# Attention ahead of a mixture of experts: softmax sums from a column of ones, logit sums on GpSimd

## The chip, the core and the metric

One core of one Trainium2 chip runs the whole program. The metric is the device time of one execution in microseconds (us). Five engines work side by side, each through its own queue in order: TensorE (PE, its weight loads PEld), VectorE (DVE), ScalarE (ACT), GpSimd (POOL) and SyncE (SP), which issues most DMAs.

## What is computed

Three layers follow each other on 4608 tokens (8 batches of 576) of width 512: attention with keys and values averaged over groups of 8 positions, a mixture of 8 experts of which each token takes two, and a last layer. The change lies in the first and in the gate of the second:

```python
k_p = k.reshape(B, H, Sp, 8, D).mean(axis=3)       # Sp = 72, H = 8, D = 64
v_p = v.reshape(B, H, Sp, 8, D).mean(axis=3)
scores = np.matmul(q, k_p.transpose(0, 1, 3, 2)) / np.sqrt(D)
attn = np.exp(scores - np.max(scores, axis=-1, keepdims=True))
attn = attn / (np.sum(attn, axis=-1, keepdims=True) + 1e-09)
x = np.matmul(attn, v_p)                           # heads side by side: 4608 x 512
logits = x @ w_gate                                # 8 columns
noisy = logits + np.log1p(np.exp(x @ w_noise)) * noise
top2 = np.argpartition(-noisy, 2, axis=1)[:, :2]
out[mask] += top2_w * (np.maximum(x[mask] @ w1[e], 0.0) @ w2[e])
h = out @ w_in;  result = (h - np.tanh(h)) @ w_out
```

## The kernel before

`attention()` works on 36 tiles of 128 tokens. Nothing reorders its instructions: each engine runs them in the order in which the Python code emits them. The loop at L1665 goes over steps t, and in one step several tiles are at different stages: the exponentials of tile t (`st_exps`), the transposes of the weights of tile t-2 (`st_attT`), the transposes of q of tile t+2 (`st_q`), the scores and their row maxima of tile t+1 (`st_scores`), the product of the weights with V of tile t-3 (`st_av`), and the scaling of that product of tile t-4 (`st_g`).

`VB` holds V with 64 columns a head and, behind them, 16 more: V times the gate's weights `w_gate` and `w_noise`, so that one product gives a head's part of x and its part of the 16 logits, 80 columns a head. It is made once a batch by `vscale` (L1274): on VectorE the scales, the logit part (L1287) and the copies of the scale to `isc` (L1293, L1295); on GpSimd, for batches 2 to 7, the V part (L1299). GpSimd also halves K and V of later batches (L1146), for VectorE to go on with.

The exponentials run on ScalarE, eight a tile (one a head), each with the row's sum as a second result (`accum_out`), for which the trace shows a second instruction, ACTIVATION_READ_ACCUMULATOR. `st_norm` adds 1e-9 to the sums of four tiles at once and takes their reciprocals on VectorE (L1353, L1356). `st_g` then scales on VectorE: the x columns from PSUM into `xr` (L1404), which goes to memory by DMA, and the 128 logit columns into `lg` (L1412). At the end of every group of `sums` (five tiles, one of four, one of two) a VectorE sum over the heads gives `lz` (L1414). The product with V lies in one PSUM buffer, `px`, except for tiles 33 and 35, which use two others, and so two scalings each.

The gate (`gate_jobs`, L1430) works on groups of 10, 10, 9 and 7 tiles, that is when `st_g` has ended tiles 9, 19, 28 and 35, in steps 13, 23, 32 and 39. It is a generator: `tick()` emits its next VectorE operation, at fixed places between the stages of a step. Its first is `lz * isc` (L1442), its second two ScalarE operations on the result (L1443, L1444). It ends in lists of the tokens of each expert (`lists`), built by VectorE, ScalarE and TensorE.

Of the kernel before, what the change touches and what calls it, by code (L numbers as in the profile page):

```python
# [10 lines left out]
F32 = mybir.dt.float32  # L11
# [3 lines left out]
AF = mybir.ActivationFunctionType  # L15
OP = mybir.AluOpType
AX = mybir.AxisListType
# [1097 lines left out]
def attention(nc, tc, st, V):  # L1115
    q, k, v, w_gate, w_noise, noise = (V[n] for n in ("q", "k", "v", "w_gate", "w_noise", "noise"))
    B, H, S, D, N, E, DM, SP, NT, HP = (V[n] for n in ("B", "H", "S", "D", "N", "E", "DM", "SP", "NT", "HP"))
# [7 lines left out]
    ts = nc.vector.tensor_scalar  # L1125
# [18 lines left out]
    def add(e, b, nm, n, c=slice(0, 5)):  # L1144
        a = KV[b, nm]
        e.tensor_add(a[:, c, 0:n], a[:, c, 0:n], a[:, c, n:2 * n])  # L1146
# [37 lines left out]
    rowi = one.tile([128, 128], F32, name="rowi")  # L1184
    nc.gpsimd.iota(rowi, pattern=[[1, 128]], base=0, channel_multiplier=-1, allow_small_or_imprecise_dtypes=True)
    KB = [one.tile([128, 2 * HP * SP], F32, name=f"kb{i}") for i in range(2)]
    VB = [one.tile([128, 5, 3, D + 2 * E], F32, name=f"vb{i}") for i in range(2)]

    of = one.tile([128, 5, 4], F32, name="of")
    odd = one.tile([128, 5, 2], F32, name="odd")  # L1190
# [44 lines left out]
    def head_mask():  # L1235
        ts(lm, hm, float(SP), 8.0, op0=OP.is_lt, op1=OP.mult)
        ts(hm, hm, 0.0, None, op0=OP.is_ge)
        tt(hm, hm, lm, op=OP.mult)

    def prep_jobs(b, first=False):  # L1240
        tl = {}

        def k2():
            add(nc.vector, b, "k", 2)

        def k1():
            add(nc.vector, b, "k", 1)
            tl["ke"] = wk.tile([128, 5, 2, D], F32, name="ke", bufs=1)
            tt(tl["ke"], KV[b, "k"][:, :, 0:1].to_broadcast([128, 5, 2, D]), odd[:, :, :, None].to_broadcast([128, 5, 2, D]),
               op=OP.mult)  # L1250

        def v2():
            add(nc.vector, b, "v", 2)

        def v1():
            add(nc.vector, b, "v", 1)
            tl["va"] = KV[b, "v"]
            tl["vm"] = wk.tile([128, 1], F32, name="vm")
            nc.vector.tensor_reduce(tl["vm"], tl["va"][:, :, 0], axis=AX.XY, op=OP.max, apply_absolute_value=True)

        def vmaxT():
            p = ps.tile([1, 128], F32, name="pt", bufs=3)
            nc.tensor.transpose(p, tl["vm"], identf)
            q = [ps.tile([64, 4, 128], F32, name="pt", bufs=3) for _ in range(2)]
            for c in range(5):
                nc.tensor.transpose(q[c // 4][:, c % 4], tl["va"][:, c, 0], identf)
            yield
            tl["vx"] = wk.tile([1, 1], F32, name="vx")
            nc.vector.tensor_reduce(tl["vx"], p, axis=AX.X, op=OP.max)
            tl["vT"] = wk.tile([64, 5, 128], F32, name="vT", bufs=1)  # L1270
            nc.scalar.activation(tl["vT"][:, 0:4], q[0], AF.Copy)
            nc.scalar.activation(tl["vT"][:, 4], q[1][:, 0], AF.Copy)

        def vscale():  # L1274
            p = ps.tile([128, 1], F32, name="pt", bufs=3)
            nc.tensor.matmul(p, ones1, tl["vx"], start=True, stop=True)
            vg = ps.tile([128, 5, 3, 2 * E], F32, name="pt", bufs=3)
            for c in range(5):
                nc.tensor.matmul(vg[:, c].rearrange("p j e -> p (j e)"), tl["vT"][:, c],
                                 wg[:, hb[c]:hb[c] + 3].rearrange("p h e -> p (h e)"), start=True, stop=True)  # L1280
            yield
            m = wk.tile([128, 3], F32, name="vs")
            pow2(nc, m, p)
            of8 = wk.tile([128, 5, 3], F32, name="of8")
            ts(of8, hm, m[:, 2:3], None, op0=OP.mult)
            vb, bc = VB[b % 2], lambda n: of8[:, :, :, None].to_broadcast([128, 5, 3, n])
            tt(vb[:, :, :, D:], vg, bc(2 * E), op=OP.mult)  # L1287
            lo, hi = b * S, b * S + S
            t0, t1 = lo // 128, -(-hi // 128)
            for t in range(t0, t1):  # L1290
                o0, o1 = max(lo - 128 * t, 0), min(hi - 128 * t, 128)
                if o1 - o0 < 128:
                    ts(isc[o0:o1, t:t + 1], m[o0:o1, 1:2], 1.0 / 128, None, op0=OP.mult)  # L1293
            f0, f1 = -(-lo // 128), hi // 128
            ts(isc[:, f0:f1], m[:, 1:2].to_broadcast([128, f1 - f0]), 1.0 / 128, None, op0=OP.mult)  # L1295
            e, cs = (nc.gpsimd, each) if b > 1 else (nc.vector, [(0, 5)])
            for c0, c1 in cs:
                s = slice(c0, c1)
                e.tensor_tensor(vb[:, s, :, 0:D], tl["va"][:, s, 0:1].to_broadcast([128, c1 - c0, 3, D]), bc(D)[:, s], op=OP.mult)  # L1299

        def kbd():
            for i, (c0, c1) in enumerate(((0, 3), (3, 5))):
                w = cuts[c1] - cuts[c1 - 1]
                p = ps.tile([128, 4, 128], F32, name="pt", bufs=3)[:, 0:c1 - c0, 0:w]
                for c in range(c0, c1):
                    nc.tensor.transpose(p[:, c - c0], tl["ke"][:w, c].rearrange("p i d -> p (i d)"), identf[:w, :w])
                o = KB[b % 2][:, cuts[c0]:cuts[c1]].rearrange("p (c n) -> p c n", n=w)
                nc.scalar.activation(o, p, AF.Copy, scale=1.0 / 512)
            yield
        return dict(k2=k2, k1=k1, v2=v2, v1=v1, vt=vmaxT, vs=vscale, kb=kbd)  # L1310

    QT, SC, AT, ATT, PV, XT, SM, RC = {}, {}, {}, {}, {}, {}, {}, {}

    def st_q(t):
        p = ps.tile([128, HP, 128], F32, name="pt", bufs=3)
# [19 lines left out]

    def st_exps(t):
        at = wk.tile([128, 2, 4, SP], F32, name="at", bufs=3)
        if t % 4 == 0:
            SM[0] = wk.tile([128, 4, 2, 4], F32, name="sm"), t
        sm, t0 = SM[0]  # L1340
        AT[t] = at
        for g, (p, mx) in enumerate(SC.pop(t)):
            for j in range(4):
                nc.scalar.activation(at[:, g, j], p[:, j], AF.Exp, bias=mx[:, j:j + 1], accum_out=sm[:, t - t0, g, j:j + 1])
        if t % 4 == 3:
            SM[1] = sm, t0

    def st_norm(t):
        if t % 4 != 3:
            tick(2)  # L1350
            return
        sm, t0 = SM.pop(1)
        ts(sm, sm, 1e-9, None, op0=OP.add)  # L1353
        tick()
        rc = wk.tile([128, 4, H], F32, name="rc")
        nc.vector.reciprocal(rc, sm.rearrange("p t a b -> p t (a b)"))  # L1356
        for u in range(t0, t + 1):
            RC[u] = rc[:, u - t0]
        tick()

    def st_attT(t):
        at = AT.pop(t)
        a = wk.tile([128, 5, 128], F32, name="aT")
# [9 lines left out]
    def st_av(t):  # L1373
        a = ATT.pop(t)
# [3 lines left out]
            p = ps.tile([128, 2, 512], F32, name="px", bufs=1)  # L1378
            p = [p[:, 0], p[:, 1], p]
        PX[t] = p  # L1380
        n1 = D + 2 * E
        for o, n, b, s in runs(t):
            vb = VB[b % 2]
            for g, parts in enumerate((((0, 0, 2), (1, 0, 3), (2, 0, 1)), ((2, 1, 2), (3, 0, 2), (4, 0, 2)))):
# [5 lines left out]

    PX = {}
    sums = (0, 5, 10, 15, 20, 25, 29, 34)
    LG = [None, 0]

    def st_g(t):
        p, rc = PX.pop(t), RC.pop(t)
        xr = wk.tile([128, DM], F32, name="xr", bufs=3)
        r = rc.rearrange("p (g h) -> p g h", g=2)[:, :, :, None]
        n1 = 4 * (D + 2 * E)
        gs = [(slice(0, 2), p[2][:, :, 0:n1].rearrange("p g (h n) -> p g h n", h=4))] if len(p) == 3 else \  # L1400
            [(slice(g, g + 1), p[g][:, 0:n1].rearrange("p (g h n) -> p g h n", g=1, h=4)) for g in range(2)]
        for g, x in gs:
            m = x.shape[1]
            tt(xr.rearrange("p (g h n) -> p g h n", g=2, h=4)[:, g], x[:, :, :, 0:D], r[:, g].to_broadcast([128, m, 4, D]), op=OP.mult)  # L1404
        nc.sync.dma_start(x_d[128 * t:128 * t + 128, :], xr)
        if t in sums:
            LG[0] = wk.tile([128, 5, 2, 4, 2 * E], F32, name="lg", bufs=2)
            LG[1] = t
        lg, t0 = LG
        for g, x in gs:  # L1410
            m = x.shape[1]
            tt(lg[:, t - t0, g], x[:, :, :, D:], r[:, g].to_broadcast([128, m, 4, 2 * E]), op=OP.mult)  # L1412
        if t + 1 in sums or t + 1 == NT:
            nc.vector.tensor_reduce(lz[:, t0:t + 1], lg[:, 0:t + 1 - t0].rearrange("p t g h e -> p t e (g h)"),  # L1414
                                    axis=AX.X, op=OP.add)

    def psum(shape):
        return ps.tile(shape, F32, name="pt", bufs=3)
# [116 lines left out]
    def tick(n=1):  # L1535

        while pend and n and held[0] != "pe":
            n -= 1
            if held[0]:
                held[0] -= 1  # L1540
            else:
                step_gate()
# [122 lines left out]
    for t in range(NT + 4):  # L1665
# [7 lines left out]
        if t >= NT:  # L1673
            warm(4, "psc")
        if 0 <= t - 1 < NT:
            st_norm(t - 1)
        if 0 <= t - 4 < NT:
            st_g(t - 4)
            if t - 4 in groups:
                pend.append(gate_jobs(*groups[t - 4]))  # L1680
        tick()
        if 0 <= t - 2 < NT:
            st_attT(t - 2)
        if t + 2 < NT:
            st_q(t + 2)
        tick()
# [73 lines left out]
```

## Time and profile before

| | us |
|---|---|
| median of 3 runs (lowest to highest) | 1770.16 (1767.76 to 1774.76) |
| the profiled execution | 1768.31 |
| its span, from first to last instruction | 1766.5 |
| busy in it: TensorE, weight loads | 1724.0, 1037.9 |
| busy in it: VectorE, ScalarE, GpSimd | 1285.0, 922.6, 277.0 |

Times in the rows count from the start of the span. The attention stage is the first 217 us or so; the first matmul of the experts on gathered tokens starts at 217.16. A busy time is the time covered by an engine's records; records of one engine overlap a little, so the spacing of starts says more of what a short operation costs than its own time. Where an instruction waited, the row says for which engine and line.

### The profile page before, as it was taken

The page shows a single profiled execution, that of the slowest core. Times are in us where ns is not written, and L with a number is a line of the kernel's source. Part 1 is how long each engine was busy: PE and PEld are TensorE (multiplying, and loading weights), DVE is VectorE, ACT ScalarE, POOL GpSimd, SP SyncE. Part 2 cuts the span into 40 slices and gives each one's busy share as a digit, 9 for nine tenths or more (in the row PEclk, how much of TensorE's full clock was granted, in tenths as well). Part 3 has the DMA queues.
Part 4 walks back from the last instruction along what each step waited for, and adds up shares of the span by engine and source line. Part 5 has one row for each costly group of instructions (what it writes and reads, how often), then busy time and mean ns, then how long its engine had stood idle before and what let it go on. Part 6 is the DMA issues. An engine that isn't in the chain of part 4 may idle for free. (4 is left out here: it accounts for less than half of the span.)

```text
span 1766.5 us, 28298 instructions
## 1 busy us (share of the span) xinstructions
PE 1724.0 (98%) x10456; PEld 1037.9 (59%) x10456; DVE 1285.0 (73%) x2566; ACT 922.6 (52%) x2229; POOL 277.0 (16%) x291
## 2 busy tenths in 40 slices
PE   8988899999999999999999999999999999999998
PEld 6988744455454545545454544666666666666664
DVE  7899867766667676666564558688787879788765
ACT  6887624434343443424243356466575757666554
POOL 3343113022030301101010111012020101110000
PEclk9999999999999999999999999999999999999999
DMA  9967334644755565554553435242231414131100
GB/s 249 274 174 199 97 101 133 164 129 138 223 135 158 139 146 149 140 134 123 155 144 81 125 94 147 55 90 69 46 93 39 88 27 96 36 79 53 33 25 26
DMA packets 264127, 203.44 MB, mean 115 GB/s; under 512 B 188129, under 2 KB 208609, under 8 KB 263969
## 3 DMA queue, kind: packets, MB, share of 16 engines
q1 hardware_dynamic: 251808, 162.16, 34.8%
q0 software_dynamic: 11904, 38.81, 8.5%
q8 instruction: 87, 1.43, 0.3%
q14 instruction: 72, 0.58, 0.1%
q10 hardware_dynamic: 256, 0.46, 0.1%
HBM read 121.82 MB, written 45.74 MB: 95 GB/s over the span
## 5 line engine op out<-in xcount | busy, mean ns | idle before, releaser
L360 ACT ACTIVATE hT<-ph 128x512 f16<-128x512 f32 (+2 forms) x192 | 96.9, 505 | 438.8 <-PE ph L358 427.9
L356 PE MATMUL ph<-xTp,pair 128*128 128x384 f16 (+2 forms) x736 | 245.5, 334 | 1.1 <-PEq L456 0.6
L357 PE MATMUL ph<-xTp,pair 128*128 128x384 f16 (+2 forms) x736 | 245.0, 333 | 1.6 <-issue 1.6
L358 PE MATMUL ph<-xTp,pair 128*128 128x384 f16 (+2 forms) x736 | 245.1, 333 | 0.0
L361 DVE SCALAR_TENSOR_TENSOR hT<-ph,hT 128x512 f16<-128x512 f32 (+2 forms) x192 | 110.8, 577 | 179.5 <-ACT hT L360 176.1
L1047 PE MATMUL py<-wo,gT 128*128 128x512 f16 x576 | 218.4, 379 | 1.0 <-issue 1.0
L1045 PE MATMUL py<-wo,gT 128*128 128x512 f16 x576 | 218.4, 379 | 0.1
L379 PE MATMUL py<-pair,hT 128*128 128x512 f16 x576 | 218.4, 379 | 0.0
L1046 PE MATMUL py<-wo,gT 128*128 128x512 f16 x576 | 218.4, 379 | 0.0
L380 PE MATMUL py<-pair,hT 128*128 128x512 f16 x576 | 218.4, 379 | 0.0
L378 PE MATMUL py<-pair,hT 128*128 128x512 f16 x576 | 218.4, 379 | 0.0
L904 PEld LDWEIGHTS <-wi 128*128 128x128 f16 x1536 | 150.2, 98 | 59.0 <-DMA y<-yp 0.9
L315 POOL DMA_INDIRECT xg<-x_d,idx x75 | 78.7, 1050 | 667.2 <-DVE xp L342 510.3
L718 POOL DMA_INDIRECT y<-y_d,ridx x64 | 78.8, 1232 | 519.0 <-DVE y L729 240.7
L356 PEld LDWEIGHTS <-pair 128*128 128x128 f16 x768 | 75.3, 98 | 76.3 <-issue 15.8
L357 PEld LDWEIGHTS <-pair 128*128 128x128 f16 x768 | 75.4, 98 | 58.7 <-issue 2.9
L358 PEld LDWEIGHTS <-pair 128*128 128x128 f16 x768 | 75.4, 98 | 57.0 <-issue 1.1
L1004 ACT ACTIVATE th<-th,bias 128x512 f32<-128x512 f32 x144 | 102.5, 711 | 3.3 <-DVE th L1002 1.6
L1005 DVE SCALAR_TENSOR_TENSOR th<-th,t 128x512 f32<-128x512 f32 x144 | 98.8, 686 | 1.4 <-ACT th L1004 1.4
L1001 DVE SCALAR_TENSOR_TENSOR t<-hb,cinf,hs 128x512 f32<-128x512 f32 x64 | 48.0, 750 | 70.8 <-ACT hs L1000 68.7
L994 DVE TENSOR_TENSOR gT<-th,gT 128x512 f16<-128x512 f32 x144 | 98.9, 687 | 0.2 <-ACT gT L993 0.2
L1047 PEld LDWEIGHTS <-gT 128*128 128x128 f16 x576 | 56.3, 98 | 69.3 <-issue 1.5
(317 smaller groups left out, 3429.3 us busy)
## 6 DMA issues: line engine op xcount, KB each, us to landing
stage<-in_moe_w SPq DMA_DIRECT2D x64, 512.0 KB
y_d<-ys SPq DMA_DIRECT2D x82, 256.0 KB
x_d<-xr SPq DMA_DIRECT2D x36, 256.0 KB
out<-o SPq DMA_DIRECT2D x36, 256.0 KB
qt<-in_q SPq DMA_DIRECT2D x32, 256.0 KB
raw<-in_moe_w_in SPq DMA_DIRECT2D x32, 256.0 KB
raw<-in_moe_w_out SPq DMA_DIRECT2D x32, 256.0 KB
kt<-in_k SPq DMA_DIRECT2D x7, 768.0 KB
```

The costliest lines, as they stand in the source:

```text
L356: nc.tensor.matmul(p[:, :nt], w[:, 0, m, s], x[:, 0, m, :nt], start=(m == 0), stop=False)
L357: nc.tensor.matmul(p[:, :nt], w[:, 0, m, s], x[:, 1, m, :nt], start=False, stop=False)
L358: nc.tensor.matmul(p[:, :nt], w[:, 1, m, s], x[:, 0, m, :nt], start=False, stop=(m == KD - 1))
L361: stt(h[:, 1, :nt], p[:, :nt], 0.0, h[:, 0, :nt], op0=OP.max, op1=OP.subtract)
L378: nc.tensor.matmul(p, h[:, 0, s], w[:, 0, f], start=(f == 0), stop=False)
L379: nc.tensor.matmul(p, h[:, 0, s], w[:, 1, f], start=False, stop=False)
L380: nc.tensor.matmul(p, h[:, 1, s], w[:, 0, f], start=False, stop=(f == KF - 1))
L904: nc.tensor.matmul(p, w[:, a, m], y[:, c, b, m], start=(start and m + x == 0), stop=(m == 1 and x == 2), skip_group_check=True)
L1004: nc.scalar.activation(q, q, AF.Square, bias=bias[:, 2:3], scale=SP5)
L1045: nc.tensor.matmul(p, g[:, 0, s], wo[:, 0, f], start=(f == 0), stop=False)
L1046: nc.tensor.matmul(p, g[:, 0, s], wo[:, 1, f], start=False, stop=False)
L1047: nc.tensor.matmul(p, g[:, 1, s], wo[:, 0, f], start=False, stop=(f == KF - 1))
```

## The change

V's buffer gets an 81st column a head, which holds one where the row belongs to the head: the product with V then gives the sum of a row's exponentials beside x and the logits. The exponentials run without `accum_out`, `st_norm` goes, and `st_g` adds 1e-9 and takes the reciprocals for each tile by itself, reading the sums from PSUM. ScalarE copies the unscaled logit columns into `lg` (`st_lg`, which comes after `st_attT`), and GpSimd scales those of a whole group of `sums` with the reciprocals kept in `rc` and adds up the eight heads by halves. Tiles 34 and 35 are scaled and summed on VectorE as before. The copies to `isc` go to GpSimd. A group of the gate is put in the list after `st_lg`.

```diff
-    VB = [one.tile([128, 5, 3, D + 2 * E], F32, name=f"vb{i}") for i in range(2)]
+    VB = [one.tile([128, 5, 3, D + 2 * E + 1], F32, name=f"vb{i}") for i in range(2)]
...
+        for vb in VB:
+            ts(vb[:, :, :, D + 2 * E:], hm[:, :, :, None], 0.125, None, op0=OP.mult)
...
-                    ts(isc[o0:o1, t:t + 1], m[o0:o1, 1:2], 1.0 / 128, None, op0=OP.mult)
+                    nc.gpsimd.tensor_scalar(isc[o0:o1, t:t + 1], m[o0:o1, 1:2], 1.0 / 128, None, op0=OP.mult)
...
-            ts(isc[:, f0:f1], m[:, 1:2].to_broadcast([128, f1 - f0]), 1.0 / 128, None, op0=OP.mult)
+            nc.gpsimd.tensor_scalar(isc[:, f0:f1], m[:, 1:2].to_broadcast([128, f1 - f0]), 1.0 / 128, None, op0=OP.mult)
...
-                nc.scalar.activation(at[:, g, j], p[:, j], AF.Exp, bias=mx[:, j:j + 1], accum_out=sm[:, t - t0, g, j:j + 1])
+                nc.scalar.activation(at[:, g, j], p[:, j], AF.Exp, bias=mx[:, j:j + 1])
...
-        n1 = D + 2 * E
+        n1 = D + 2 * E + 1
...
     def st_g(t):
+        if t in sums:
+            LG[0:3] = [wk.tile([128, 5, 8 * n], F32, name=s, bufs=2) for s, n in (("lg", 2 * E), ("rc", 1))] + [t]
+        t0 = LG[2]
+        sm = wk.tile([128, H], F32, name="sm")
+        rc = LG[1][:, t - t0]
...
+        for g, x in gs:
+            ts(two(sm)[:, g], x[:, :, :, D + 2 * E:], 1e-9, None, op0=OP.add)
+        nc.vector.reciprocal(rc, sm)
...
+    def st_lg(t):
+        gs, r = LX.pop(t)
+        lg, rc, t0 = LG
+        o = lg[:, t - t0].rearrange("p (g h e) -> p g h e", g=2, h=4)
+        n = t + 1 - t0
+        done = t + 1 in sums or t + 1 == NT
+        last = t >= sums[-1]
+        for g, x in gs:
+            y = x[:, :, :, D:D + 2 * E]
+            if last:
+                tt(o[:, g], y, r[:, g].to_broadcast([128, x.shape[1], 4, 2 * E]), op=OP.mult)
+            else:
+                nc.scalar.activation(o[:, g], y, AF.Copy)
+        if done and last:
+            nc.vector.tensor_reduce(lz[:, t0:t + 1], lg[:, 0:n].rearrange("p t (h e) -> p t e h", h=H), axis=AX.X, op=OP.add)
+        elif done:
+            l, add = lg.rearrange("p t (h e) -> p (t h) e", h=H), nc.gpsimd.tensor_add
+            nc.gpsimd.tensor_tensor(l[:, 0:H * n], l[:, 0:H * n],
+                                    rc.rearrange("p t h -> p (t h)")[:, 0:H * n, None].to_broadcast([128, H * n, 2 * E]), op=OP.mult)
+            for h in (4, 2):
+                add(lg[:, 0:n, 0:2 * E * h], lg[:, 0:n, 0:2 * E * h], lg[:, 0:n, 2 * E * h:4 * E * h])
+            add(lz[:, t0:t + 1], lg[:, 0:n, 0:2 * E], lg[:, 0:n, 2 * E:4 * E])
...
         if 0 <= t - 1 < NT:
-            st_norm(t - 1)
+            tick(2)
         if 0 <= t - 4 < NT:
             st_g(t - 4)
-            if t - 4 in groups:
-                pend.append(gate_jobs(*groups[t - 4]))
         tick()
         if 0 <= t - 2 < NT:
             st_attT(t - 2)
+        if 0 <= t - 4 < NT:
+            st_lg(t - 4)
+            if t - 4 in groups:
+                pend.append(gate_jobs(*groups[t - 4]))
```

## Rows read from the trace of the kernel before

**Rows 1.** Stretches: length, then busy PE, PEld, DVE, ACT, POOL, clock, DMA share, GB/s.

```profile
30.00:70.00 40.00, 39.95 (x320) 37.48 (x319) 33.31 (x73) 34.81 (x178) 20.20 (x27) 1.00 1.05 278
70.00:190.00 120.00, 106.11 (x840) 98.33 (x839) 110.43 (x276) 94.42 (x449) 44.87 (x64) 0.97 0.68 185
190.00:210.00 20.00, 20.00 (x165) 18.53 (x164) 16.74 (x56) 13.68 (x53) 3.28 (x5) 1.00 0.26 93
...
250.00:1766.50 1516.50, 1499.63 (x8835) 850.95 (x8833) 1074.02 (x2008) 755.86 (x1474) 201.91 (x176) 1.00 0.40 103
```

**Rows 2.** Waits from 70 to 190 us: who waited for whom, total, times, longest.

```profile
ACT at L1344 <- DVE mx L1331: 9.9, 8, 3.8
...
PE px L1387 <- DVE lg L1412: 6.3, 4, 3.6
...
PE pt L1276 <- ACT aT L1370: 2.4, 2, 1.7
```

**Rows 3.** Stretches of a lower granted clock, the first and the last of three.

```profile
85.40:88.90 3.50, 3.50 (x16) 3.32 (x15) 2.47 (x8) 1.18 (x8) 3.33 (x7) 0.51 0.99 314
...
215.20:222.00 6.80, 4.84 (x12) 1.80 (x13) 3.41 (x11) 0.83 (x1) 0.00 (x0) 0.50 0.35 117
```

**Rows 4.** Groups by line, 0 to 218 us: busy, mean ns, idle before.

```profile
L1356 DVE RECIPROCAL rc<-sm 128x32 f32<-128x32 f32 x9 | 3.1, 347 | 0.2
...
L1353 DVE TENSOR_SCALAR sm<-sm 128x32 f32<-128x32 f32 x9 | 2.6, 291 | 0.0
...
L1295 DVE TENSOR_SCALAR isc<-vs 128x4 f32<-128x4 f32 x8 | 2.3, 286 | 0.1
...
L101 DVE TENSOR_SCALAR vs<-pt 128x1 f32<-128x1 f32 x8 | 1.2, 150 | 0.0
...
L1272 ACT ACTIVATE vT<-pt 64x128 f32<-64x128 f32 x8 | 2.1, 259 | 0.0
```

**Rows 5.** Timeline of VectorE in step 13: start, length.

```profile
76.92 0.68 DVE L1404 TENSOR_TENSOR xr<-px,rc 128x512 f32<-128x512 f32 x1
77.52 0.28 DVE L1412 TENSOR_TENSOR lg<-px,rc 128x128 f32<-128x128 f32 x1
77.83 1.25 DVE L1414 TENSOR_REDUCE lz<-lg 128x80 f32<-128x640 f32 x1
```

**Rows 6.** Timeline of GpSimd around step 23.

```profile
118.16 5.70 POOL L1146 TENSOR_TENSOR kt<-kt 128x256 f32<-128x256 f32 x5 [0.64 <-DMA kt<-in_k]
138.92 2.37 POOL L1299 TENSOR_TENSOR vb<-vt,of 128x192 f32<-128x192 f32 x5 [15.06 <-PE pt L1369]
141.26 3.46 POOL L1146 TENSOR_TENSOR vt<-vt 128x256 f32<-128x256 f32 x5
```

**Rows 7.** Timeline of ScalarE and TensorE in step 13, in brackets the wait before.

```profile
74.44 0.32 ACT L1344 ACTIVATE at<-psc,mx 128x72 f32<-128x72 f32 x1 [0.72 <-DVE mx L1331]
74.66 0.19 ACT L1344 ACTIVATION_READ_ACCUMULATOR at<-psc,mx 128x1 f32 x1
...
76.82 0.77 ACT L1370 ACTIVATE aT<-pt 128x384 f32<-128x384 f32 x2
...
78.60 1.88 PE L1387 MATMUL px<-vb,aT 128*128 128x160 f32 x12
...
83.50 0.38 PE L1276 MATMUL pt<-vx,onec 1*128 1x1 f32 x2 [0.74 <-ACT aT L1370]
```

**Rows 8.** Timeline of VectorE and TensorE around the second and third gate group.

```profile
135.72 1.22 DVE L1414 TENSOR_REDUCE lz<-lg 128x80 f32<-128x640 f32 x1
...
144.75 1.34 DVE L1146 TENSOR_TENSOR vt<-vt 128x640 f32<-128x640 f32 x1 [0.62 <-POOL vt L1146]
...
149.67 4.63 PE L1387 MATMUL px<-vb,aT 128*64 128x160 f32 x24 [3.56 <-DVE lg L1412]
...
185.98 1.04 DVE L1414 TENSOR_REDUCE lz<-lg 128x64 f32<-128x512 f32 x1
```

**Rows 9.** The group of the products with V, 0 to 218 us.

```profile
L1387 PE MATMUL px<-vb,aT 128*128 128x160 f32 (+5 forms) x456 | 72.9, 319 | 6.3 <-DVE lg L1412 6.3
```

## What is predicted

> **What bounds the kernel now.** I read first the busy time of each engine by stretches [rows 1]. From 250 us on, TensorE is busy 1499.6 of 1516.5 us with work the change doesn't touch, so only the attention stage, some 217 us, can move. From 30 to 70 us TensorE is busy 39.95 of 40 us: freeing another engine there gains nothing. From 70 to 190 us VectorE is busy 110.4 of 120 us, TensorE 106.1 and ScalarE 94.4: VectorE is the fullest, and TensorE stands still for about 14 us. From 190 to 210 us TensorE is full again. The list of waits of the middle stretch [rows 2] says what ends these 14 us: 6.3 us wait for the logit product of VectorE (L1412, which frees the one `px` buffer), 2.4 us (two waits) for ScalarE's copy L1370; the rest are smaller pieces. So a microsecond off VectorE between 70 and 190 us is worth up to a microsecond; off ScalarE, a part of 2.4 us; elsewhere nearly nothing. Last the granted clock: in three spells TensorE ran at 1.2 instead of 2.4 GHz, two of 3.4 us and one of 6.8 us [rows 3]; each 3.4 us spell costs 1.7 us of full-speed work.
>
> **VectorE, removed.** The mean times are in [rows 4], the spacing of starts in [rows 5]. A logit product ends 0.20 us after the x product before it (77.80 against 77.60): it holds the engine 0.20 us. Those of 34 of the 36 tiles go (the last two keep theirs): 6.9 us. Of eight sums L1414 seven go, six of 1.25 us and one of 1.04 [rows 5, 8]: 8.5 us. The batched add and reciprocal, 9 x (0.29 + 0.35): 5.7 us. The scale copies L1295 and L1293, which go to GpSimd, 8 x (0.29 + about 0.15, as L101): 3.5 us. In all 24.6 us.
>
> **VectorE, added.** Each tile gets its own add and reciprocal on 8 columns, two adds where the PSUM buffer is split (tiles 33 and 35). The add is nearest to L101, one column from PSUM, 0.15 us, 0.18 with the gap of a dependent one. The reciprocal lies between 0.15 (one column) and 0.35 (32 columns); a quarter of the way up, with the gap, 0.24. 38 x 0.18 + 36 x 0.24 = 15.5 us; from both sides, at 0.15 each 11 us, at 0.29 and 0.35 (the 32-column times) 23.6 us. Without the sums, 16.1 go and 15.5 come: nothing per tile. So VectorE's gain is the seven sums, and it comes in steps of 1.25 us, one every five tiles.
>
> **The new wait.** Three of these seven (tiles 9, 19, 28) close a group of the gate, and the next VectorE operation after them is `lz * isc` (L1442). Now VectorE stands at it until ScalarE has copied the tile's logits and GpSimd has done four dependent operations: 640 columns multiplied, then 320, 160 and 80 added. GpSimd's prices [rows 6]: 192 columns with a broadcast operand take 2.37/5 = 0.47 us, 256 added 3.46/5 = 0.69, and 5.70/5 = 1.14 where VectorE worked beside them. By the first the 1200 columns make 3.0 us, by the last 5.3; I take 3.2, the undisturbed rows with the hand-overs, since VectorE itself stands still meanwhile (in the third group 960 columns, 2.6).
>
> The Trainium skill ("GPSIMD Engine Reference", When to use GPSIMD, Engine selection) speaks against this move: two-input elementwise work belongs on VectorE, GpSimd being about half as fast. Its 2.6 cycles an element at 1.2 GHz would make 2.6 us of the 1200 columns before dispatch, an estimate; the rows agree with the direction, and the sum by it would be half a microsecond lower a group.
>
> Group 1, in step 13 [rows 5, 7]: the copies L1370 start at 76.82 and last 0.77, the logit copy after them some 0.26 (a 128-column copy, L1272), so GpSimd starts at about 77.95 and is done by 81.2; VectorE has ended its x product by 78.0 (76.92 + 0.42 + 0.68). L1442, which followed the sum that ended at 79.08, starts at 81.3: 2.2 us later, 3.3 us of standing. Behind it on VectorE lie the maxima of tile 14. ScalarE waits too: L1443 in its queue needs the same result, and behind that are the exponentials of tile 14, which free the score banks, and the copies for which TensorE already waited 0.74 us at 83.50. TensorE has no cover: +2.2.
>
> Group 2, in step 23: VectorE's sum starts at 135.72 and ends at 136.94 [rows 8]. GpSimd is idle until 138.92 [rows 6], so by the same steps L1442 starts at 138.7: +1.7. This delay runs on through GpSimd's queue: `vb` (138.92), then the five adds at 141.26, for which VectorE waited at 144.75 [rows 8]; the scale copies now on GpSimd add some 0.3 before `vb`. From there VectorE arrives late at L1412, for which TensorE stood 3.56 us at 149.67. +2.0 in all.
>
> Group 3, in step 32: the sum started at 185.98 and took 1.04 us [rows 8]; L1370 ends at about 187.0 and GpSimd at 190.0, so L1442 is 2.5 us late. There TensorE is full (190 to 210 us), and VectorE has pauses; I charge 0.5. Between the groups one sum goes without a wait, in steps 18 and 28: -1.25 each. That of step 8 lies where TensorE is full: 0. That of step 37 is balanced by adds and reciprocals of the last three tiles, done before in one batch at 202 us: 0.
>
> **ScalarE.** The 288 reads of the accumulator go. Eight exponentials with them span 76.82 - 74.44 = 2.38 us, while a read starts 0.22 after its exponential [rows 7]; 8 x 0.22 = 1.76 us leaves 0.6 us a tile, less 0.26 for the logit copy. Most exponentials start the moment the maximum is there (9.9 us of waits [rows 2]), so ScalarE is not the limit; the two TensorE waits on L1370 [rows 2] shrink by 0.6 each: -1.2.
>
> **TensorE.** Each head is 81 columns instead of 80: 1.25% of 72.9 us [rows 9] and of the 3.8 us in the last buffers, +0.9. **The `px` buffer** is freed by ScalarE too, after the copies L1370 of the same step; the product with V started 0.6 us or more after these in nearly all steps (78.60 against 77.59 in step 13 [rows 7]), the copy needs 0.26, and ScalarE is earlier: 0. The two mask operations at the start lie where VectorE waits for scores: 0. GpSimd's other four sums come in steps where it waits anyway: 0.
>
> **Sum.** 2.2 + 2.0 + 0.5 - 2.5 - 1.2 + 0.9 = +1.9, of which 0.3 is given back by faster logit hand-over in group 2 and 3 (ScalarE's exponentials end 0.6 earlier there): +1.6. The profiled execution took 1768.31 us (span 1766.5), the median is 1770.16, 1.85 more: 1769.9 for such an execution, 1771.8 as a median.
>
> **Rivals.**
> *The waits are covered* (0.18). If GpSimd's chain is near 2 us, or the gate's first operation finds its result ready, VectorE loses nothing and keeps three more sums. Then: -2.5 - 3 - 1.2 + 0.9, and with the small operations at 0.15 another -2.5 (20 of 36 tiles lie in the stretch it bounds), one clock spell less -1.7: 1760 to 1766. For it: VectorE is what TensorE waits for. Against: GpSimd's own rows allow no chain under 3 us.
> *The waits are long* (0.17). GpSimd works at its disturbed price, 5.3 us a chain: +2.1 for each of three groups, little of it covered, and the delayed `vb` and adds keep VectorE waiting; with small operations nearer 0.3 (+4 in the stretch bounded by VectorE) and one more clock spell (+1.7) the time is 1778 to 1784. It decides from a chain of about 4.5 us. For it: the five adds at 118.16 took 5.70 us beside VectorE's work. Against: VectorE is idle in just these chains. The Trainium skill ("SBUF — State Buffer", SBUF: two separate sides) says that a VectorE operation with two SBUF inputs and a GpSimd operation that reads SBUF exclude each other for a whole instruction; the row at 118.16 agrees with it, and the other four sums, which meet a working VectorE, would be slowed so.
> *It doesn't free VectorE at all* (0.05): a reciprocal of 8 columns costs what one of 32 does; 8 us come on VectorE, about 4.5 of them in its stretch: 1776.
>
> **How the numbers follow.** The forecast itself has 0.60, with 1768 to 1776 as its own spread. Half a per cent, 8.9 us, is about what a measurement of this kernel tells from no change. The first rival passes that bound in less than half of its cases: faster 0.07. The second in most: slower 0.13. The same: 0.80. The range takes in most of both: 1763 to 1782.
>
> **What would show it.** After: on VectorE a pause of about 3 us before each of the first three L1442, ended by GpSimd; four GpSimd operations of together 3 us a group, at seven places; no sums of 1.25 us but one short one; adds of about 0.15 and reciprocals of 0.2 us, 36 tiles of them; exponentials following each other at about 0.22 us. It would be wrong if L1442 starts with no pause, if TensorE's pauses between 70 and 190 us move away from 14 us by more than 5, or if a clock spell comes or goes.

## The result and the profile after

The changed kernel takes 1785.75 us (median; 1784.89 without one disturbed run, which the comparison leaves out), the kernel before 1768.41 us beside it: ratio 1.0086, 95% interval 1.0067 to 1.0104, or about 15 us more (12 to 18). The prediction was 1771.8 us, 1763 to 1782, so the time lies above the range. The profiled execution took 1786.61 us with a span of 1784.8, against 1768.31 and 1766.5. Of the signs that were to show the prediction wrong two came: TensorE's pauses between 70 and 190 us grew from 13.9 to 19.7 us, by more than 5, and a spell of the lower clock came, four from 70 us on instead of three.

First by stretches, in the columns of [rows 1]; the stretch from 70 us to the first matmul of the experts is shown for both kernels. After:

```profile
30.00:70.00 40.00, 39.04 (x309) 36.28 (x309) 33.07 (x72) 29.94 (x111) 24.72 (x33) 1.00 0.97 264
70.00:190.00 120.00, 100.31 (x759) 90.99 (x759) 98.64 (x245) 75.33 (x261) 58.72 (x87) 0.94 0.64 181
70.00:236.00 166.00, 137.80 (x1057) 124.64 (x1056) 135.08 (x359) 100.61 (x342) 72.29 (x106) 0.95 0.54 155
250.00:1784.80 1534.80, 1516.01 (x8924) 858.78 (x8922) 1088.94 (x2061) 760.66 (x1481) 202.73 (x176) 1.00 0.40 104
```

Before, the same stage:

```profile
70.00:218.00 148.00, 129.88 (x1029) 119.46 (x1028) 134.90 (x354) 109.47 (x502) 48.15 (x68) 0.97 0.60 166
```

The experts start 18 us later (235.25 against 217.2 us), and what lies behind their start takes 1549.6 us in this profile and 1549.4 in that of before: between these two the loss is all in the attention stage. VectorE, which the change was to free, does as much there as before, 135.1 against 134.9 us, and stands still for 30.9 us instead of 13.1. TensorE stands 28.2 instead of 18.1 us. It is also busy 7.9 us longer; about 3 of these are work that a later start pushed past 70 us, and the granted clock was 0.95 on the mean instead of 0.97. GpSimd's work went from 48 to 72 us.

Who waited for whom after, from 70 to 236 us (total, times, longest), against [rows 2]:

```profile
ACT lg L1414 <- DVE xr L1396: 16.0, 13, 6.1
...
DVE lz L1450 <- POOL lz L1423: 10.6, 3, 3.7
...
ACT g_th L1451 <- DVE lz L1450: 9.2, 3, 3.2
...
PE px L1370 <- ACT lg L1414: 7.7, 4, 5.1
PE pt L1521 <- DVE l_row L1516: 7.6, 4, 3.4
...
DVE vt L1146 <- POOL vt L1146: 2.0, 1, 2.0
```

The first two did not exist before; the third was 3.2 us in two waits. The second is the stop that the prediction priced. The first is one that it did not see: ScalarE's logit copy waits for VectorE's x product, although both only read the one `px` buffer. Held by it are `px` itself and all that is queued on ScalarE behind the copy. That TensorE waits 7.7 us for `px` instead of 6.3 is not by itself the copy's price: `e4_ones_only`, which has no such copy, shows 8.5 (below).

VectorE's groups of the stage (columns as [rows 4]):

```profile
L1392 DVE RECIPROCAL rc<-sm 128x8 f32<-128x8 f32 x36 | 7.3, 203 | 1.2
L1391 DVE TENSOR_SCALAR sm<-px 128x8 f32<-128x8 f32 x34 | 5.4, 159 | 11.6 <-PE px L1370 11.4
...
L1450 DVE TENSOR_TENSOR lz<-lz,isc 128x160 f32<-128x160 f32 (+1 forms) x3 | 1.0, 321 | 10.6 <-POOL lz L1423 10.6
```

The add and the reciprocal last about what was forecast (0.16 and 0.20 us). Step 13, the place of [rows 5, 7], from the timelines of the three engines:

```profile
80.10 0.69 DVE L1396 TENSOR_TENSOR xr<-px,rc 128x512 f32<-128x512 f32 x1
84.46 0.33 DVE L1450 TENSOR_TENSOR lz<-lz,isc 128x160 f32<-128x160 f32 x1 [3.67 <-POOL lz L1423]
...
80.83 0.28 ACT L1414 ACTIVATE lg<-px 128x128 f32<-128x128 f32 x1 [0.66 <-DVE xr L1396]
...
84.82 0.27 ACT L1451 ACTIVATE g_th<-lz 128x80 f32<-128x80 f32 x1 [3.23 <-DVE lz L1450]
...
81.18 1.28 POOL L1419 TENSOR_TENSOR lg<-lg,rc 128x640 f32<-128x640 f32 x1 [4.35 <-ACT lg L1414]
82.54 1.46 POOL L1422 TENSOR_TENSOR lg<-lg 128x320 f32<-128x320 f32 x2
84.08 0.35 POOL L1423 TENSOR_TENSOR lz<-lg 128x80 f32<-128x80 f32 x1
```

The chain is the one forecast: GpSimd needs 3.25 us (81.18 to 84.43), VectorE stands 3.67 us, ScalarE 3.23. The delay against before grows in steps: the products with V are 3 us late up to tile 10, 6 to 9.4 at tiles 14 to 18, 11 to 14 at tiles 21 to 24, 16 at tiles 30 to 35.

### The profile page after: what moved, and what is told of

It reads as the page before. It is cut to its first block, busy times and chain, and to the rows that moved or that the text cites. A ratio compares the mean times of both kernels' runs of the same rounds, so it can differ in the third digit from the quotient of the medians.

```text
span 1784.8 us, 28071 instructions
## 1 busy us (share of the span) xinstructions
PE 1727.8 (97%) x10456; PEld 1039.9 (58%) x10456; DVE 1283.5 (72%) x2566; ACT 906.6 (51%) x1976; POOL 305.7 (17%) x335
```

## The experiments

A kernel's excess is its ratio less one, times 1768 us, in the form excess [interval]; the change itself has +15 [12, 18]. "Start" is the first matmul of the experts in a profile: 217.2 us before, 235.2 after. The two measures need not agree: what lies behind the start took 1545.7 to 1552.9 us in the profiles of kernels that don't touch it, 1547.7 to 1549.6 in three of the kernel before. So where they differ, both are given.

**The column of ones alone.** `e4_ones_only` leaves logits and sums on VectorE.

```diff
-        last = t >= sums[-1]
+        last = True
```

> Only the first part of the change: sums of the softmax by the column of ones, an add and a reciprocal for each tile, the scale copies on GpSimd; the logit columns are scaled and summed by VectorE for all tiles, as before the change. Neither ScalarE's copy nor GpSimd's sums are there. If these two carry the loss, the time is that of the kernel before within 5 us (1764 to 1774). If the adds and reciprocals of each tile and the 81st column cost what is lost, it stays above 1780.

Measured: 1777.42 us, +10 [7, 13], start 225.87. A large part of the loss, 10 of 15 us by the ratios and 8.7 of 18.1 by the starts, comes without GpSimd's sums and without ScalarE's copy.

**Without most of the adds and reciprocals.** `e7_ones_one_reciprocal` is that kernel with one pair for each block of tiles.

```diff
-        rc = LG[1][:, t - t0]
+        rc = LG[1][:, 0]
...
-        for g, x in gs:
+        if t == t0:
+            for g, x in gs:
```

> The first part alone (column of ones, logits on VectorE), but the add and the reciprocal are done for the first tile of every group of tiles alone and used for all of them: 28 of 36 pairs are left out, so the output isn't scaled rightly. It takes 28 x 0.43 = 12 us off VectorE. If the small operations are what the first part costs, the time falls from 1777.4 to that of before, give or take 2 us (1766 to 1770), or below. If the 81st column, the exponentials without sums or the start cost it, it falls by under 3 us.

Measured: 1771.73 us, +2 [0, 5], start 222.35. The 28 pairs that are gone are 28 x (0.16 + 0.20 + 0.07 of gaps) = 12 us of VectorE, and they cost 7.6 us by the ratios (uncertain by some 4) and 3.5 by the starts. What is left has 5.8 us less on VectorE than the kernel before (batched add and reciprocal 5.7 and scale copies 3.5 gone, eight pairs of 0.43 come), and is no faster for it; but its scale copies bring a wait of their own, as is shown further down.

**The wider buffer.** `e6_before_pad` is the kernel before with 128 unused bytes, `e12_change_pad` the changed one with 384.

```diff
+    pad = one.tile([128, 32], F32, name="pad")
```

> The kernel before, with 128 unused bytes a partition laid behind V's buffers, as much as the 81st columns take there; no instruction changes. In all five profiles with the wider buffer TensorE waits 4.8 to 5.7 us for the loads of q at the start, against 3.0 in the one profile before. If the place of the buffers behind them slows those loads, the waits are about 5 us here too and the time rises by about 2 us. If not (chance in the one profile before, or another part of the change), they stay near 3 us and the time is that of before within 1 us.

> The changed kernel with 384 unused bytes a partition behind V's buffers, so that together with the 81st columns the buffers behind lie 512 bytes further than before the change instead of 128. If the place of the buffers slows the loads at the start, TensorE waits about 3 us for q there, as before, and the time falls by about 2 us (1783 to 1784). If the place has no part in it, the wait stays at 4.8 us or more, and the time too.

Measured: 1771.05 us, +2 [0, 4], start 220.89; and 1785.15 us, +15 [11, 20], start 233.97. So e6 and e7 agree: all that e7 changes adds up to no more than an idle pad does. At the very start TensorE waits 5.7 us for `q` after, in two pieces, and 3.1 in `e12_change_pad`; the two pieces after:

```profile
21.04 1.11 PE L1320 MATMUL pt<-identf,qt 128*128 128x128 f32 x4 [4.32 <-DMA qt<-in_q]
...
27.94 0.63 PE L1320 MATMUL pt<-identf,qt 128*128 128x128 f32 x4 [1.40 <-DMA qt<-in_q]
```

The shorter wait gained nothing in the time, so the wait for `q` is not the cause by itself.

**Repeats.** `e15_before_again` and `e16_before_again2` are the kernel before, `e17_change_again` and `e18_change_again2` the changed one, each once more.

> The kernel before, unchanged, profiled once more. If TensorE's wait for q at the start (3.0 us in the one profile before, 4.2 to 5.7 in most others, 1.5 in one) belongs to the kernel, it is within 0.5 us of 3.0 again. If it varies from execution to execution, it is not. The same for the spells of low clock: four before, of together 17 us up to the start of the experts.

> As the one above, a third profile of the kernel before: wait for q at the start within 0.5 us of 3.0 if it belongs to the kernel, spread by over 1 us if it varies.

> The changed kernel, unchanged, profiled once more. If the wait for q at the start (5.7 us) and the spells of low clock (24 us in all) belong to the kernel, they come again within 0.5 and 3.4 us; the start of the experts is then again 18 us later than before, within 2.

> As the one above, a third profile of the changed kernel: 5.7 us of waiting for q and 24 us of low clock if they belong to the kernel; the three stops before the gate, 3.2 to 3.7 us each, come again in any case.

Measured: 1768.95 and 1768.97 us, starts 217.5 and 219.4; 1790.79 and 1786.76 us, starts 236.1 and 234.7. The later start by 15 to 19 us is there in every pair. The stretches of lower granted clock are not: up to 10 us past the experts' start they add up to 17.1, 17.1 and 27.3 us before and 23.9, 41.0 and 27.3 after, and the profile with 41 us starts the experts only 0.9 us later than the one with 23.9. The wait for `q` varies too, 0.7 to 3.0 us before and 3.6 to 5.7 after.

**The gate's sums off GpSimd.** `e10_gate_sums_vectore` lets VectorE scale and sum for tiles 9, 19 and 28, and leaves GpSimd the other four sums.

```diff
-        if done and last:
+        if done and t in (9, 19, 28):
+            l = lg.rearrange("p t (h e) -> p (t h) e", h=H)
+            tt(l[:, 0:H * n], l[:, 0:H * n],
...
+            nc.vector.tensor_reduce(lz[:, t0:t + 1], lg[:, 0:n].rearrange("p t (h e) -> p t e h", h=H), axis=AX.X, op=OP.add)
+        elif done and last:
```

> The changed kernel, but the scaling and sum of the three groups that the gate reads at once (tiles 9, 19 and 28) is done by VectorE; the other four stay on GpSimd. VectorE's three stops of 3.2 to 3.7 us give way to 2.05 us of work each. If the stops cost as the attention stage of the kernel with the later gate says (6 us), a part of 3 to 5 us comes back and the time is 1778 to 1781. If a stop and the same time of work cost the same, it is 1782 to 1784.

Measured: 1780.16 us, +9 [6, 13], start 230.42; no stop before `lz * isc`. The three stops cost 4.8 us by the starts, 5.8 by the ratios, more than the three times 1.94 us of work that VectorE does in their place.

**The gate one step later.** `e2_gate_one_step_later` gives the chain a step of time.

```diff
-            if t - 4 in groups:
-                pend.append(gate_jobs(*groups[t - 4]))
+            u = t - 4 if t - 4 == NT - 1 else t - 5
+            if u in groups:
+                pend.append(gate_jobs(*groups[u]))
```

> The changed kernel, with one edit: a group of the gate (but the last) is put in the list one step, some 5 us, later, so that GpSimd's sums are ready before VectorE reads them. If the three stops of VectorE (3.67, 3.67 and 3.21 us) are what costs, they are gone and the time falls by 5 to 8 us. If ScalarE's copy behind VectorE is what costs, the time moves by less than 3 us, and ScalarE's waits for the x product stay at 15 to 20 us.

Measured: 1783.19 us, +15 [11, 18]. The stops are gone, and the experts start 6.5 us earlier than after. But the rest takes 1553.5 us instead of 1549.6; 3.23 us of it are a wait for the gathered tokens (`xg`) that the changed kernel doesn't have. From its timeline of TensorE:

```profile
228.73 0.58 PE L356 MATMUL ph<-x0T,pair 128*128 128x512 f16 x1 [6.53 <-DVE lg L1412]
...
272.63 0.63 PE L333 MATMUL pt<-identf,xg 128*128 128x128 f32 x4 [3.23 <-DMA xg<-x_d,idx]
```

**The logit copy on VectorE.** `e1_copy_vectore` copies the raw logits there and leaves the rest of the change.

```diff
-                nc.scalar.activation(o[:, g], y, AF.Copy)
+                nc.vector.tensor_copy(o[:, g], y)
```

> The changed kernel, with one edit: the unscaled logit columns are copied from PSUM by VectorE instead of ScalarE. Theory A (ScalarE's copy has to wait for VectorE's x product out of the same PSUM buffer, 18.5 us in 16 waits, and holds back everything behind it on ScalarE and the release of px): these waits are gone, TensorE's waits for the copy (7.7 us) become shorter ones for VectorE, and in spite of 0.2 us a tile more on VectorE the time falls by 4 to 9 us of the 17 lost. Theory B (the three stops of VectorE before the gate, and its operations slowed beside GpSimd's sums, are the whole loss): VectorE has 7 us more to do and the time stays or rises, 0 to +5 us.

Measured: 1783.10 us, +16 [13, 19], start 234.39: no difference. Handing the logit columns from VectorE to ScalarE was worth nothing. ScalarE's wait at the copy has only moved to its next place on VectorE, the maxima (waits from 70 to 235 us):

```profile
ACT at L1343 <- DVE mx L1333: 14.0, 13, 3.9
...
PE px L1370 <- DVE lg L1414: 7.4, 4, 4.0
```

**All sums on VectorE.** `e3_sum_vectore` keeps ScalarE's copy and gives GpSimd none of the seven sums.

```diff
-            nc.gpsimd.tensor_tensor(l[:, 0:H * n], l[:, 0:H * n],
...
+            tt(l[:, 0:H * n], l[:, 0:H * n],
...
+            nc.vector.tensor_reduce(lz[:, t0:t + 1], lg[:, 0:n].rearrange("p t (h e) -> p t e h", h=H), axis=AX.X, op=OP.add)
```

> The changed kernel, with one edit: the scaling and the sum over heads of a group of tiles are done by VectorE (one multiplication of 640 columns, about 0.8 us, and the sum of 1.25 us) and not by GpSimd. It puts 7 x 2 = 14 us on VectorE. If the wait for GpSimd and the slowing of VectorE's operations beside GpSimd are the loss, both are gone: VectorE's stops before the gate vanish, and the time falls by 2 to 6 us net of the 14. If ScalarE's copy is the loss, VectorE is later still, its copies wait longer, and the time rises by 3 to 10 us.

Measured: 1787.92 us, +22 [18, 26], start 233.1. Against `e4_ones_only` this kernel has nearly the same work on VectorE (141.6 and 139.2 us from 70 us to the experts), and is 10.5 us slower in the median (7.2 by the starts). The two differ in two things: ScalarE copies the logits, and scaling and sum come in one burst of 2 us. TensorE's waits from 45 us on, first in `e3_sum_vectore`, then in `e4_ones_only`:

```profile
PE px L1370 <- ACT lg L1414: 7.7, 4, 5.1
PE pt L1519 <- DVE l_row L1514: 7.4, 3, 4.1
PE pt L1278 <- ACT aT L1353: 3.0, 1, 3.0
...
PE pt L1268 <- ACT qT L1322: 1.9, 2, 1.6
PE pt L1268 <- ACT g_e L1469: 1.1, 1, 1.1
PE pt L1352 <- ACT vT L1273: 1.1, 1, 1.1
```

```profile
PE px L1370 <- DVE lg L1412: 8.5, 4, 5.1
PE pt L1521 <- DVE l_row L1516: 5.6, 4, 3.1
...
PE pt L1278 <- ACT aT L1353: 2.6, 1, 2.6
...
PE pt L1352 <- ACT vT L1273: 0.6, 1, 0.6
```

`px` itself is not waited for longer; the new waits are for what stands behind the copy in ScalarE's queue (`qT`, `g_e`, `vT`). How the loss divides between that queue and the burst was not separated. Beside `e10_gate_sums_vectore` it says something else: the two differ only in four of the sums, some 8 us of VectorE's work, which there are GpSimd's, and e10 is faster by 12.6 us by the ratios, 7.8 by the medians, 2.7 by the starts. With ScalarE's copy in place, taking these sums off VectorE did pay, by an amount that is not settled.

**GpSimd busy for nobody.** `e8_ones_idle_sums` is `e4_ones_only` with the four operations of seven sums done on a buffer that nobody reads.

```diff
+    LS = one.tile([128, 5, 16 * E], F32, name="ls")
...
+            if t < sums[-1]:
+                l, add = LS.rearrange("p t (h e) -> p (t h) e", h=H), nc.gpsimd.tensor_add
```

> The first part alone, and beside it GpSimd does the four operations of each of seven sums on a buffer of its own, whose result nobody reads; the real sums are VectorE's. It adds to the first part only GpSimd's being busy: VectorE's operations beside it, and what waits in GpSimd's queue. If VectorE's being slowed beside GpSimd (0.17 us operations that took 1.23 us) carries a large part of the loss, the time rises by 3 to 6 us over the first part alone (1777.4). If it carries little, by less than 1.5 us.

Measured: 1778.97 us, +8 [5, 12], start 231.29. In the profile the stage is 5.4 us longer than in `e4_ones_only`; in the time the two can't be told apart (1.6 us by the medians, none by the ratios), since the part behind came out 3.9 us shorter. VectorE's and GpSimd's operations around step 18, first in `e4_ones_only`, then here:

```profile
103.94 4.13 POOL L1146 TENSOR_TENSOR vt<-vt 128x256 f32<-128x256 f32 x5 [6.04 <-PE pt L183]
...
111.26 0.83 DVE L1251 TENSOR_TENSOR ke<-kt,odd 128x640 f32<-128x640 f32 x1
112.00 1.28 DVE L159 SCALAR_TENSOR_TENSOR pair<-stage,wsc,pair 128x1024 f16<-128x1024 f32 x1
...
113.42 0.57 DVE L1513 TENSOR_TENSOR l_one<-slot,g_col 128x800 f16<-128x800 f16 x1
```

```profile
111.26 5.57 POOL L1146 TENSOR_TENSOR vt<-vt 128x256 f32<-128x256 f32 x5
...
112.66 1.24 DVE L1251 TENSOR_TENSOR ke<-kt,odd 128x640 f32<-128x640 f32 x1
113.83 1.74 DVE L159 SCALAR_TENSOR_TENSOR pair<-stage,wsc,pair 128x1024 f16<-128x1024 f32 x1
...
116.24 1.02 DVE L1524 TENSOR_TENSOR l_one<-slot,g_col 128x800 f16<-128x800 f16 x1
```

What VectorE meets here are not the added operations but GpSimd's old additions L1146, which come 7 us later here, behind the added ones, and meet VectorE at work.

**Work taken off the kernel before.** `e9_before_four_sums` moves four sums and the scale copies to GpSimd; `e14_before_no_sums` takes the accumulator reads off ScalarE and leaves out the softmax's sums.

```diff
-                nc.scalar.activation(at[:, g, j], p[:, j], AF.Exp, bias=mx[:, j:j + 1], accum_out=sm[:, t - t0, g, j:j + 1])
+                nc.scalar.activation(at[:, g, j], p[:, j], AF.Exp, bias=mx[:, j:j + 1])
```

> The kernel before, with two parts of the change alone, those for which nothing waits at once: the sums over heads of tiles 4, 14, 24 and 33 are done by GpSimd (three adds by halves, of columns that VectorE has scaled as before), and the scale copies are GpSimd's. It takes 5 + 3.4 us off VectorE without a column of ones, a copy by ScalarE or a stop before the gate. If VectorE's work is what counts and GpSimd's costs nothing, the time falls by 3 to 6 us below that of before (1763 to 1766). If VectorE's operations are slowed beside GpSimd by as much, it is that of before within 2 us.

> The kernel before without the sums of the exponentials: no accum_out, so no reads of the accumulator, and the sums' buffer is set to a constant by GpSimd once in four tiles; the softmax isn't divided by its sums. It gives ScalarE back 0.6 us a tile and changes nothing else. By the prediction's step on ScalarE the time falls by 1 to 2 us. If ScalarE bounds more than the waits say, it falls by 4 us or more.

Measured: 1769.83 us, +1 [-2, 3], start 219.59; and 1771.04 us, +3 [0, 6], start 218.2. Neither gains, though e9 has some 8.4 us less on VectorE. No kernel of the study beats the one before.

## Why the prediction was wrong

**The account.** By the ratios, +2 up to the buffer and the column (e7, and e6 with the pad alone), +7.6 for an add and a reciprocal in every tile (e4 less e7), +5.3 for logits and sums on ScalarE and GpSimd (the change less e4): 15. Each of the two differences is uncertain by some 4 us, as the intervals give it. The profiles' starts, 222.35, 225.87 and 234.7 to 236.1 us, order the three in the same way, but make the second part 3.5 us and the third 9 to 10. So both parts are there, and which is the larger is not settled.

**The step that failed** is "16.1 go and 15.5 come: nothing per tile". Both amounts are right as lengths, and VectorE's busy time in the stage is the same. But the 15.5 us cost: the 12 of them that e7 leaves out are worth 3.5 to 7.6. What was taken off gained nothing that could be measured: the logit products 6.9 us (e1), batched add, reciprocal and scale copies 9.2 us (e7, e9), ScalarE's reads (e14, where -1.2 was forecast). Full busy time had been read as if each microsecond counted the same, 110.4 of 120 [rows 1]. Why the pairs cost and the rest doesn't pay stays open. An add and a reciprocal stand ahead of the x product, and TensorE waits until logits and x product have left `px`; but from e7 to e4 the wait for `px` grows by 0.9 us only (7.6 to 8.5), as much as those for the lists, for `idx` and for the copies `aT` do (about 1 us each). No run moved the same work from one place to the other.

**The scale copies hide a cost.** Around step 24 VectorE waits for GpSimd's additions 0.62 us in all five profiles in which the scale copies are VectorE's, and 1.3 to 4.8 us in eleven of the twelve in which they are GpSimd's; TensorE's wait for `px` that follows is 3.55 to 3.81 and 4.01 to 5.13 us. (The twelfth, `e17_change_again`, has 0.62 and 3.64.) The copies stand ahead of `vb` in GpSimd's queue, as the prediction says; it put 0.3 us on that. So e7 and e9 don't show that work off VectorE is worth nothing: a gain of one or two microseconds may be hidden behind this wait.

**"The `px` buffer: 0" failed too.** The copy's own time was right (0.28 us, 0.26 forecast); that it must wait for VectorE's x product was missed: 16.0 us in 13 waits. The Trainium skill ("PSUM — Partial Sum Buffer", PSUM bank collisions raise a hardware error) says that two engines may not touch one bank in the same partitions at once, two readers included, and that the compiler orders them. The 13 waits agree: two readers of `px` run one after the other. By that rule the logit copy stays in VectorE's chain whichever engine does it, and e1, which gives it back to VectorE, measures no difference.

**Stops: right in size.** Before `lz * isc` VectorE stood 3.67, 3.67 and 3.21 us (forecast: 3.3 in step 13). Their cost was put at 4.7 us and comes out at about 5 (4.8 to 5.8 in e10, beyond the work that takes their place there; 6.5 in e2, by the start). That the second delay runs on through GpSimd's queue is not shown. VectorE does wait for GpSimd's late additions, 2.00 us instead of 0.62 [rows 8], and TensorE 5.10 instead of 3.56 us:

```profile
156.33 1.34 DVE L1146 TENSOR_TENSOR vt<-vt 128x640 f32<-128x640 f32 x1 [2.00 <-POOL vt L1146]
...
161.79 1.61 PE L1370 MATMUL px<-vb,aT 128*64 128x162 f32 x4 [5.10 <-ACT lg L1414]
```

But `e4_ones_only`, where no stop comes before, has the same two waits, and e10 has them too:

```profile
148.38 1.33 DVE L1146 TENSOR_TENSOR vt<-vt 128x640 f32<-128x640 f32 x1 [1.99 <-POOL vt L1146]
...
153.88 5.51 PE L1370 MATMUL px<-vb,aT 128*64 128x162 f32 x24 [5.11 <-DVE lg L1412]
```

**The sums of steps 18 and 28 (-2.5)** were to be pure gain. GpSimd's operations meet a VectorE at work, and both get longer. What is left of the gain no run shows by itself: e9 has them, two more and the scale copies on GpSimd and gains nothing, and e10 gains by its four against `e3_sum_vectore`. Step 18 after:

```profile
113.00 1.28 POOL L1419 TENSOR_TENSOR lg<-lg,rc 128x640 f32<-128x640 f32 x1 [12.15 <-ACT lg L1414]
...
113.09 1.23 DVE L1494 TENSOR_TENSOR g_e<-g_e,g_hi 128x20 f32<-128x20 f32 x1
...
114.36 2.42 POOL L1422 TENSOR_TENSOR lg<-lg 128x320 f32<-128x320 f32 x2
...
115.02 1.38 DVE L1251 TENSOR_TENSOR ke<-kt,odd 128x640 f32<-128x640 f32 x1
...
116.32 1.54 DVE L159 SCALAR_TENSOR_TENSOR pair<-stage,wsc,pair 128x1024 f16<-128x1024 f32 x1
...
116.86 1.21 POOL L1423 TENSOR_TENSOR lz<-lg 128x80 f32<-128x80 f32 x1
```

An operation on 20 columns lasts 1.23 us (0.16 in `e4_ones_only`), GpSimd's two adds 2.42 (1.46 in step 13) and its 80-column add 1.21 (0.35). Summed over the operations that both kernels have, VectorE's are 4 to 7 us longer in the three profiles of the change than in the first of before (1.5 longer in the second of before), and no longer in `e4_ones_only`. The Trainium skill's rule of the shared port ("SBUF — State Buffer", SBUF: two separate sides), weighed as part of the second rival, agrees: the 20-column operation starts 0.09 us after GpSimd's multiplication and ends within 0.05 us of its end.

**The rival of long waits** (0.17, 1778 to 1784) came nearest in time, and half in cause: it had the slowing of the other four sums, but the gate's chains themselves stayed at the undisturbed 3.2 us. It and the third rival did put 4 and 4.5 us on the adds and reciprocals, but by longer durations, and the durations came out as forecast. That these amounts lie near the measured cost is luck.

**Open.** About 2 us of the late start go with a wider buffer, with no cause shown: in the twelve profiles with one (e6 and e7 among them) the x product of tile 0 starts 1.6 to 3.9 us later than in the first profile of before, in the four others 0.3 us earlier to 1.8 later. The sum had no term for it. What GpSimd's mere presence costs lies between nothing and 5.4 us (e8). The lower clock differs from execution to execution by more than between the kernels.

## What to carry to other kernels

Don't cancel work added to the fullest engine against work taken off it: ask for each piece what waits behind it at its own place, and count neither at its full length until a wait in the trace changes with it. Before splitting the emptying of one PSUM buffer over two engines, count it as a chain of the two. A step moved to GpSimd must find a consumer that comes later, a VectorE that is not at work, and nothing behind it in GpSimd's own queue that another engine waits for.

## What was unexpected of the hardware

Two engines that only read one PSUM buffer run one behind the other in this program (13 waits, 16.0 us, for copies of 0.28 us). The largest loss of a VectorE operation beside GpSimd that the lines above show fell on a short one: 0.16 us became 1.23, about the length of the GpSimd operation beside it (1.28), while a 1024-column one went from 1.28 to 1.54. Not all suffer: an addition of 320 columns took 0.47 us beside GpSimd (`e8_ones_idle_sums`) and without it (`e4_ones_only`). A reciprocal of 8 columns takes 0.20 us against 0.35 for 32 [rows 4], so a batch of four tiles costs 0.35 where four single ones cost 0.81.
